# Gated linear attention into a softplus MLP: paired first blocks worked by halves of the heads, and the bias additions moved

## The chip, the cores and the metric

The kernel runs on one core of a Trainium2 chip. The metric is device time in microseconds (us) of one launch; the mean granted clock of TensorE was 0.99 of full or more in every run compared here, unless a run is called slow. Each run was timed beside runs of the kernel before on the same chip.

The engines carry short names in the profile: PE is TensorE (matmul), PEld its weight loads, DVE is VectorE, ACT is ScalarE, POOL is GpSimd, SP is SyncE, which issues the loads and stores. A name such as L474 is line 474 of the kernel that was profiled; the changed kernel has other line numbers for the same work.

## The reference

```python
batch, n_heads, seq, head_dim = (4, 8, 768, 48)      # q, k, v, f_logit: f32
n_tokens, d_model, d_ff = (3072, 384, 2048)          # w_in, w_out: f32

f = 1.0 / (1.0 + np.exp(-f_logit))
for t in range(S):
    state = f[:, :, t, :, None] * state + np.einsum('bhd,bhe->bhde', k[:, :, t], v[:, :, t])
    y[:, :, t] = np.einsum('bhd,bhde->bhe', q[:, :, t], state)
x = y.transpose(0, 2, 1, 3).reshape(B * S, H * D)
h = x @ w_in
g = np.maximum(h, 0.0) + np.log1p(np.exp(-np.abs(h)))
out = (g @ w_out).astype(np.float32)
```

## The kernel before

The 3072 tokens are 24 blocks of 128, six to a batch. Per block the attention is done in chunked form: the cumulative sum of the log gate is a matmul (`cs`), its exponentials scale k and q (`ek`, `eq`, then the products `mk` and `mq`), TensorE transposes the products (`tr`), multiplies them (`p`), VectorE masks the result (`m`, the tile `ptm`), and the output (`o`) is the masked part plus the state's part. The state is carried by `u`, `tt` and `sn`. Then x is transposed (`xt`) and goes through 48 matmuls with w_in (`f1`), exp, ln, and 16 matmuls with w_out (`f2`).

All engines execute their queues in order, and the program decides the order once, when it is built: every piece of work is a task with an engine, a guessed cost, the tasks it needs and a key, and a small list scheduler lays the tasks out. The first four blocks are loaded as two pairs, so that one 384 KB load brings even and odd tokens of two blocks:

```python
def load(n, i):
    b, c = divmod(i, NC)
    if i < PAIRED:
        t = work.tile([128, H, 2, D], FP32, name=n + "2", tag=n + "2", bufs=2)
        nc.sync.dma_start(out=t, in_=SRC[n][b, :, c * T:(c + 2) * T, :].rearrange(
            "h (p e) d -> p h e d", e=2))
        in_t[n, i], in_t[n, i + 1] = t[:, :, 0, :], t[:, :, 1, :]
        return
# ... [cut]
def a_cs2(i, e):                       # one block e of a pair, all heads
    ps = att_bank("cs")
    for k in range(2):
        nc.tensor.matmul(out=ps[:, 0:DM], lhsT=negS if k > e else negB,
                         rhs=z_t[i + k].rearrange("p h d -> p (h d)"), ...)
# ... [cut]
# the tasks of a pair, for each block e of it
task(("mk", i + e), "DVE", MUL, [("ek", i + e), ("k", i)], t + 2, a_mk, (i + e,), "qkp", ...)
task(("mq", i + e), "POOL", MUL, [("eq", i + e), ("q", i), ("mk", i + e)], t + 2.1,
     a_mq, (i + e,))
task(("vb", i + e), "POOL", VB, [("v", i)], t + 3, a_vb, (i + e,), "vb", ...)
# ... [cut]
# weights: each 768 KB quarter is cast in two halves of its columns
task(("cast", n, i, 0), "DVE", COPY, [("at", n, i)], key, cast_w, (n, i, 0))
task(("cast", n, i, 1), "POOL", COPY, [("at", n, i)], key + 0.1, cast_w, (n, i, 1))
# ... [cut]
# a constant from ln 2 times the column sums of w_out is added to every output row
def f_out(i):
    osb = work.tile([128, DM], FP32, name="osb", tag="osb", bufs=16)
    if i < LATE:                       # LATE = 13: copied now, added later on GpSimd
        nc.vector.tensor_copy(out=osb, in_=o_ps.pop(i)[:, 0:DM])
    else:
        nc.vector.tensor_tensor(out=osb, in0=o_ps.pop(i)[:, 0:DM], in1=bias_bc, op=ALU.add)
```

Note the three needs of `mq`: the exponential, the load of q, and `mk` of the same block, which is on another engine and which `mq` does not read.

## Time and profile before

| | before |
|---|---|
| median of the runs beside the changed kernel | 193.49 us (193.43 to 193.71, 4 runs) |
| profiled span | 191.7 us |
| TensorE busy, of it warm-up matmuls | 96%, 135 matmuls |
| first feed-forward matmul starts | 18.94 us |
| share of the chain on TensorE | 86% |

The prediction shows the lines that carry this. Columns: start, time from first start to last end, engine, line, operation, tiles, shapes, count, and in brackets how long the engine stood idle before and what ended that.

```profile
16.17 1.28 POOL L211 CAST vb<-v 128x384 bf16<-128x384 f32 x2 [3.09 <-DMA v<-in_v_dram]
18.14 1.08 POOL L211 CAST w_in_bf<-w 128x768 bf16<-128x768 f32 x1 [0.68 <-DMA w<-in_moe_w_in_dram]
...
20.65 1.84 POOL L282 TENSOR_TENSOR qkp<-q,ee 128x384 bf16<-128x384 f32 x2
```

GpSimd stands idle for 3.09 us at the cast of the second pair's v, which is at the head of its queue and waits for its load. The q products of the same pair stand behind that cast, behind a weight cast and a state update, and run only at 20.65, although the exponentials that they need were done by 15.26.

### The profile page before, as it was taken

The page shows a single profiled execution, that of the slowest core. Times are in us where ns is not written, and L with a number is a line of the kernel's source. Part 1 is how long each engine was busy: PE and PEld are TensorE (multiplying, and loading weights), DVE is VectorE, ACT ScalarE, POOL GpSimd, SP SyncE. Part 2 cuts the span into 40 slices and gives each one's busy share as a digit, 9 for nine tenths or more (in the row PEclk, how much of TensorE's full clock was granted, in tenths as well). Part 3 has the DMA queues.
Part 4 walks back from the last instruction along what each step waited for, and adds up shares of the span by engine and source line. Part 5 has one row for each costly group of instructions (what it writes and reads, how often), then busy time and mean ns, then how long its engine had stood idle before and what let it go on. Part 6 is the DMA issues. An engine that isn't in the chain of part 4 may idle for free.

```text
span 191.7 us, 6346 instructions
## 1 busy us (share of the span) xinstructions
PE 184.8 (96%) x2613; PEld 150.4 (78%) x2613; DVE 126.6 (66%) x274; ACT 149.3 (78%) x249; POOL 108.5 (57%) x154
## 2 busy tenths in 40 slices
PE   6999889999999999999999999999999999999993
PEld 6868678777887887787788788778778778788773
DVE  7847878275979778637777867556866867653011
ACT  3675497898978888899979789779789877766770
POOL 6344967069898699844345444589998533500000
PEclk9999999999999999999999999999999999999999
DMA  6999999999999963854655683687799910110112
GB/s 159 261 270 384 382 374 247 177 190 169 203 168 200 159 119 62 163 119 89 125 112 104 121 160 67 110 159 188 163 299 194 284 50 33 41 46 0 44 41 84
DMA packets 98925, 30.29 MB, mean 158 GB/s; under 512 B 92112, under 2 KB 97360, under 8 KB 98896
## 3 DMA queue, kind: packets, MB, share of 16 engines
q1 hardware_dynamic: 98896, 29.89, 71.5%
q8 instruction: 20, 0.33, 0.8%
q14 instruction: 9, 0.07, 0.1%
HBM read 25.17 MB, written 4.72 MB: 156 GB/s over the span
## 4 chain that ended last, share of the span: by engine, by line
PE 86%; SPq 4%; DMA 4%; POOL 3%; DVE 1%; issue 1%; POOLq 0%
PE hh L474 33%; PE ops L494 32%; PE qkT L296 5%; SPq L141 4%; DMA v<-in_v_dram 4%; PE pp L374 4%; PE oo L446 2%; PE xTp L460 2%; PE cs L257 2%; PE oo L441 2%; PE uu L391 1%; PE ops L501 1%; POOL qkp L282 1%; POOL sst L430 1%; POOL vb L211 1%
## 5 line engine op out<-in xcount | busy, mean ns | idle before, releaser
L474 PE MATMUL hh<-xT,w_in_bf 128*128 128x128 bf16 x1152 | 113.9, 219 | 0.6 <-DVE w_in_bf L211 0.6
L494 PE MATMUL ops<-w_out_bf,gg 128*128 128x384 bf16 x368 | 108.3, 326 | 0.0
L474 PEld LDWEIGHTS <-w_in_bf 128*128 128x128 bf16 x1152 | 87.8, 98 | 21.8 <-DVE w_in_bf L211 0.8
L482 ACT ACTIVATE uexp<-hh 128x512 f32<-128x512 f32 x96 | 56.6, 595 | 22.8 <-PE hh L474 22.0
L488 ACT ACTIVATE gg<-uexp 128x1024 bf16<-128x1024 f32 x48 | 50.7, 1056 | 1.4
L494 PEld LDWEIGHTS <-gg 128*128 128x128 bf16 x368 | 34.9, 98 | 5.2
L383 DVE TENSOR_TENSOR ptm<-pp,mask 128x512 bf16<-128x512 f32 x40 | 25.8, 686 | 7.5 <-PE pp L374 7.4
L278 POOL TENSOR_TENSOR qkp<-kk,ee 128x384 bf16<-128x384 f32 x20 | 18.3, 915 | 20.6 <-ACT ee L270 9.1
L430 POOL TENSOR_TENSOR sst<-tt,ect 48x192 bf16<-48x192 f32 x32 | 16.3, 510 | 19.4 <-DVE tt L421 15.6
L211 DVE COPY qkT<-qkT 128x1024 bf16<-128x1024 bf16 x22 | 15.2, 689 | 17.0 <-PE qkT L296 16.4
L400 DVE STREAM_TRANSPOSE ect<-ee 32x128 bf16<-32x128 bf16 x64 | 19.5, 305 | 2.5 <-ACT ee L274 1.3
L282 POOL TENSOR_TENSOR qkp<-qq,ee 128x384 bf16<-128x384 f32 x20 | 18.4, 918 | 0.0
L211 DVE CAST xx<-oo 128x384 bf16<-128x384 f32 x21 | 11.7, 557 | 6.4 <-PE oo L446 5.6
L233 POOL TENSOR_TENSOR wsum<-wsum,w 128x384 f32<-128x384 f32 x14 | 14.0, 1001 | 0.5
L525 POOL TENSOR_TENSOR osb<-osb,bias_bc 128x384 f32<-128x384 f32 x13 | 12.7, 1005 | 0.9 <-DVE bias_bc L243 0.9
L717 PE MATMUL ops<-negU,ident 128*128 128x128 bf16 x135 | 11.1, 244 | 1.9 <-POOL ident masks.py:199 1.9
L211 POOL CAST vb<-vv 128x384 bf16<-128x384 f32 x20 | 10.1, 507 | 4.5 <-DMA vv<-in_v_dram 4.5
L270 ACT ACTIVATE ee<-cs 128x384 bf16<-128x384 f32 x24 | 11.2, 477 | 1.8 <-PE cs L257 1.0
L521 DVE TENSOR_TENSOR osb<-ops,bias_bc 128x384 f32<-128x384 f32 x10 | 5.6, 558 | 10.5 <-PE ops L494 10.3
L296 PE MATMUL qkT<-ident,qkp 128*128 128x128 bf16 x160 | 12.2, 219 | 0.0
L421 DVE TENSOR_TENSOR tt<-uu,sst 48x192 f32<-48x192 f32 x32 | 11.3, 354 | 0.9
L717 PEld LDWEIGHTS <-ident 128*128 128x128 bf16 x135 | 9.6, 112 | 2.3 <-POOL ident masks.py:199 1.9
(83 smaller groups left out, 211.6 us busy)
## 6 DMA issues: line engine op xcount, KB each, us to landing
ff<-in_f_logit_dram SPq DMA_DIRECT2D x20, 192.0 KB, 4.0
kk<-in_k_dram SPq DMA_DIRECT2D x20, 192.0 KB, 3.8
qq<-in_q_dram SPq DMA_DIRECT2D x20, 192.0 KB, 4.1
vv<-in_v_dram SPq DMA_DIRECT2D x20, 192.0 KB, 4.2
out_dram<-osb SPq DMA_DIRECT2D x19, 192.0 KB, 3.0
w<-in_moe_w_in_dram SPq DMA_DIRECT2D x4, 768.0 KB, 9.2
w<-in_moe_w_out_dram SPq DMA_DIRECT2D x4, 768.0 KB, 8.8
f<-in_f_logit_dram SPq DMA_DIRECT2D x2, 384.0 KB, 5.0
```

The source lines that it names most:

```text
L211: on[eng].tensor_copy(out=out, in_=in_)
L278: on[eng].tensor_tensor(out=qkp_bufs[i % 4][:, H:2 * H, 0:D], in0=in_t.pop(("k", i)), in1=e_bufs[i % 2][:, H:2 * H, 0:D], op=ALU.mult)
L282: on[eng].tensor_tensor(out=qkp_bufs[i % 4][:, 0:H, 0:D], in0=in_t.pop(("q", i)), in1=e_bufs[i % 2][:, 0:H, 0:D], op=ALU.mult)
L296: nc.tensor.transpose(ps[:, a * 128:(a + 1) * 128], qkp[:, a, :], ident)
L383: nc.vector.tensor_tensor(out=ptm_t[i].rearrange("p (a b) t -> p b a t", b=2)[:, half, :, :], in0=p_ps.pop((i, half)).rearrange("p (a t) - ...
L400: nc.vector.transpose(out=t[32 * r:32 * r + 32], in_=e[96:128, 0:NP, 32 * r:32 * r + 32])
L430: on[eng].tensor_tensor(out=sn[lo:hi, :, e0:e0 + D], in0=tt[lo:hi], in1=ec[lo:hi].unsqueeze(2).to_broadcast([48, NP, D]), op=ALU.mult)
L474: nc.tensor.matmul(out=h_ps[i, j // 4][:, j % 4, :], lhsT=w_in_bf[:, r, j * 128:(j + 1) * 128], rhs=xT_t[i][:, r, :], start=(r == 0), stop ...
L482: nc.scalar.activation(out=u_t[i, a // 2][:, 4 * (a % 2):4 * (a % 2) + 4, :], in_=h_ps.pop((i, a)), func=AF.Exp, bias=0.0, scale=1.0)
L488: nc.scalar.activation(out=g_t[i][:, 8 * a:8 * a + 8, :], in_=u_t.pop((i, a)), func=AF.Ln, bias=0.5, scale=0.5)
L494: nc.tensor.matmul(out=o_ps[i][:, 0:DM], lhsT=g_t[i][:, j, :], rhs=w_out_bf[:, j, :], start=(j == 0), stop=(j == NJ - 1), skip_group_check ...
L717: nc.tensor.matmul(out=idle_ps[:, 0:128], lhsT=ident, rhs=negU, start=True, stop=True, skip_group_check=True)
```

## The change

The intent: let the first pairs start on half of f and pass through each step by half of the heads (both blocks of the pair together), so that the chain from load to x is shorter; and take bias work away from GpSimd late in the kernel: 8 outputs instead of 13 get their bias there, one at a time as they come, and the sums of w_out's rows that the bias needs start earlier. Some buffers become fewer. In rewriting the tasks, the change also drops the third need of `mq`. It alters more that the scheduler sees: some guessed costs, a new need among the `exp` tasks, and the engine of some copies and of some set-up work.

```diff
-SUMS = 110
-BIAS = 240
-LATE = 13
+SUMS = 64
+BIAS = 164
+LATE = 8
 ... [cut]
+            if half != 1:
+                in_t[n, i] = work.tile([128, H, 2, D], FP32, name=n + "2", tag=n + "2", bufs=2)
+            hh = slice(0, H) if half is None else slice(4 * half, 4 * half + 4)
+            nc.sync.dma_start(out=in_t[n, i][:, hh], in_=SRC[n][b, hh, c * T:(c + 2) * T, :].rearrange(
                 "h (p e) d -> p h e d", e=2))
-            in_t[n, i], in_t[n, i + 1] = t[:, :, 0, :], t[:, :, 1, :]
 ... [cut]
-    def a_cs2(i, e):
-        ps = att_bank("cs")
-        for k in range(2):
-            nc.tensor.matmul(out=ps[:, 0:DM], lhsT=negS if k > e else negB,
-                             rhs=z_t[i + k].rearrange("p h d -> p (h d)"),
+    def a_cs2(i, a):
+        ps, m = att_bank("cs"), 4 * D
+        for e in range(2):
+            for k in range(2):
+                nc.tensor.matmul(out=ps[:, e * m:e * m + m], lhsT=negS if k > e else negB,
+                                 rhs=z_t[i, a][:, k].rearrange("p h d -> p (h d)"),
 ... [cut: the same for ek, eq, products, transposes, evictions, p, masks, outputs]
-            task(("mq", i + e), "POOL", MUL, [("eq", i + e), ("q", i), ("mk", i + e)], t + 2.1,
-                 a_mq, (i + e,))
+            task(("mq", i, a), "POOL", MUL, [("eq", i, a), ("q", i)], t + 2.1, a_mul2,
+                 (i, a, "q"))
 ... [cut]
-            task(("ev", i, k), "DVE" if k else "ACT", EV, [("tr", i, k, 1)], s + 10.3, a_ev2,
+            task(("ev", i, a), "DVE", EV, [("tr", i, a, 0)], t + 10.3, a_ev2, (i, a), "qkT2",
 ... [cut]
-            task(("add", i), "POOL", 0.95, [("out", i), ("bias out",)], BIAS + 4 * i, add_bias,
+            task(("add", i), "POOL", 0.95, [("out", i), ("bias out",)], BIAS + 4 + 10 * i, add_bias,
 ... [cut]
-        task(("sum", n), "POOL", 1.08, [...], SUMS + 8 * n, add_w, (w, j))
+        task(("sum", n), "POOL", 1.08, [...], SUMS + 6 * n, add_w, (w, j))
-    slots = dict(..., vb=4, qkT=2, qkT2=3, w32=5, ptm=3, xx=2, xT=6, uexp=3, gg=6, osb=16)
+    slots = dict(..., vb=3, qkT=2, qkT2=3, w32=5, ptm=2, xx=2, xT=6, uexp=3, gg=5, osb=12)
```

## The prediction

> **What bounds the kernel now.** I read the page first, then the chain that ended last, then the timelines of the engines up to 33 us, the issue list with the landing of each load, and the start-to-start spacing of the matmuls.
>
> ```profile
> PE 184.8 (96%) x2613; PEld 150.4 (78%) x2613; DVE 126.6 (66%) x274; ACT 149.3 (78%) x249; POOL 108.5 (57%) x154
> PE   6999889999999999999999999999999999999993
> DMA  6999999999999963854655683687799910110112
> PE 86%; SPq 4%; DMA 4%; POOL 3%; DVE 1%; issue 1%; POOLq 0%
> ```
>
> TensorE carries 86% of the chain. The 96% busy flatters it, because early on it runs warm-up matmuls (line 717, 135 of them) that do nothing useful. So I count useful work instead. Back-to-back spacings in the trace are 56 ns for a 128-column matmul, 163 ns for a 384-column one, 43 ns and 25 ns for the 96- and 48-column ones. Counts times spacings give 168.3 us of useful TensorE work in the program. The last matmul ends near 188.6 us, so TensorE falls 20.3 us behind an ideal that starts at zero. Call the clock minus the useful work done by then the lag. It grows in three pieces:
>
> - to 18.94 us, where the first feed-forward matmul starts, only 5.27 us of work is done: lag 13.7;
> - at the tenth transpose of x (32.3 us) 15.24 us is done: lag 17.05, so 3.4 lost in between;
> - from there to the end another 3.3 us over 156 us, some 0.2 us per block, mostly at the p matmuls, which show two gaps of about 0.1 us per block. In 40 to 60 us the excess over nominal spacing is 1.4 us against 0.55 to 0.65 elsewhere.
>
> The chain of waits of 16 to 33 us and the timelines show what the middle piece is:
>
> ```profile
> 8.62 7.43 DMA v<-in_v_dram
> 16.17 1.28 POOL vb L211 x2
> 18.14 1.08 POOL w_in_bf L211
> 19.22 0.78 POOL sst L430
> 20.65 1.85 POOL qkp L282 x2
> 22.55 0.40 PE qkT L305 x4
> ```
> ```profile
> 18.11 0.69 DVE L211 CAST w_in_bf<-w 128x768 bf16<-128x768 f32 x1 [1.02 <-DMA w<-in_moe_w_in_dram]
> 22.47 1.34 DVE L211 CAST w_in_bf<-w 128x768 bf16<-128x768 f32 x1
> 25.50 1.22 DVE L211 CAST w_in_bf<-w 128x768 bf16<-128x768 f32 x1
> 27.40 1.89 DVE L327 TENSOR_TENSOR ptm<-pp,mask 128x512 bf16<-128x512 f32 x3
> ```
> ```profile
> 22.44 1.79 POOL L211 CAST w_in_bf<-w 128x768 bf16<-128x768 f32 x2
> ```
> ```profile
> 18.94 0.68 PE L474 MATMUL hh<-xT,w_in_bf 128*128 128x128 bf16 x9
> ```
>
> The reader should see two things. The first feed-forward matmul follows the cast of the first quarter of w_in, whose load lands at 18.08 us; x of block 0 is transposed and copied by 18.87, at the same moment. And GpSimd does the q products of the second pair only at 20.65, so half of the second weight quarter (landed 20.12) is cast only after 22.44.
>
> **What the Trainium skill says.**
> - "TensorE: Matmul & The Clock Gate", Part 1 (The HAM clock gate): about 107 ns between 128-column matmuls when cold, 56 ns after some 3.4 us of sustained work. The trace agrees: the first 43 warm-up matmuls take 4.34 us (101 ns each), later ones go at 56 ns. The change keeps warm-up matmuls, so I charge nothing for the clock.
> - "SBUF — State Buffer", SBUF: two separate sides: VectorE and GpSimd share a port pair as an exclusive lock. That fits the equal casts of 128x768 on VectorE taking 0.69 to 1.34 us, and a 128x128 copy taking 1.79 us while GpSimd clears buffers. I therefore use 0.7 to 1.2 us for such a cast.
> - "DMA: Bandwidth & Descriptors", Specifications: line rate wants descriptors of 512 B or more. The trace moves about 262 GB/s with the 384 B pieces of the pairs and 370 to 385 GB/s with the weights. The change keeps 384 B pieces, so the weights should land as before.
> - "Perfetto Trace Analysis", Identifying the Most-Contended Engine: matmul busy share is no measure of headroom. This trace agrees, as above.
>
> **The change part by part.**
>
> *Nothing in the total.* Counting matmuls of the changed program at the same spacings gives 168.3 us of useful work again. The cumulative-sum matmuls become twice as many of half the width. Warm-up matmuls fall from 135 to 102. The change can win only lag.
>
> *First pair by halves.* Half of f is 192 KB and should land near 3.7 us instead of 4.43; one half's z steps are two of about 0.5 us instead of four. I step through the new queue orders with the durations of the rows: ek of half 0 near 6.2; k landed 5.93, so mk near 6.8; q landed 7.44, so the q products on GpSimd at 7.5 to 9.3 (0.93 each); copies of qkT to 10.5 (0.69 each); four ptm products (0.69 each) with two small tt steps between, to about 13.9 instead of 16.35; outputs, x and its transposes after that, ready near 16.5 instead of 18.87. But the cast of w_in still cannot start before the landing at 18.08. So the first feed-forward matmul moves from 18.94 to about 18.85, and 2.3 us of the gain dies there.
>
> *What fills the freed time.* In the new order 32 instead of 20 qkp transposes and 48 instead of 32 p matmuls stand before the first feed-forward matmul. That is 12 x 56 ns = 0.67 us plus 16 x 21.5 ns = 0.34 us, together 1.0 us of work done in time that was warm-up. Lag there: 18.85 - 6.28 = 12.6 instead of 13.7.
>
> *From there to the 96th feed-forward matmul* (blocks 0 and 1). GpSimd has only half of vb left, near 19.0, then casts the second quarter on landing, 20.1 to 20.95, instead of 22.4. TensorE: 12 feed-forward matmuls to 19.5, the u products to 20.6, 24 more to 22.0, then quarter 3 (landed 22.11, cast on VectorE by 23.2 and on GpSimd, behind sn, by 23.75), to 24.8. Now VectorE binds: tt to 24.0, cast of quarter 4 (landed 24.18) to 25.4, and only then the last three ptm, to 27.4. The output of the first half of block 2 waits until 26.1 (1.3 us lost), that of the second half until 27.4 (0.4 lost). The rest runs through, and the 96th feed-forward matmul ends near 30.1. Useful work by the tenth x transpose is then 14.92 us at about 30.25: lag 15.3 instead of 17.05. So the two steps together win 1.75 us, 1.0 of it before the first feed-forward matmul and 0.7 after.
>
> *Blocks 4 on.* Their loads land as before (f of block 4 at 33.39, q at 35.30). In the new order the transposes of block 4 come after 24.0 us of work, at 39.3 with this lag; its q product can end near 38.6. No new wait, but little room.
>
> *Bias and sums.* 8 instead of 13 bias additions on GpSimd remove 5 x 1.005 = 5.0 us there. The evictions of blocks 8 to 12 go from a copy of 0.56 us to an addition of 0.56 us on VectorE. The 15 sums of 1.0 us are the same, only begun elsewhere in its order. GpSimd is 57% busy and off the chain: 0 us on the end. The bias matmul (0.70 us for two passes) moves on TensorE and costs the same.
>
> *Fewer buffers* (gg 6 to 5, osb 16 to 12, ptm and vb 3): 0 if the order holds. *Tail*: same final halves and stores, 0.
>
> Sum: 193.48 - 1.75 = 191.7 us.
>
> **The rivals.**
> 1. *Nothing is gained*: the head is bound by loads, 18 us of 262 to 385 GB/s; what comes early then waits at a cast or a sum. For it: the landing at 18.08 and the loss I find at VectorE. Against: 3.4 us are lost between 19 and 32 although the queue delivers a quarter every 2.05 us, and GpSimd's backlog there is plain. It would give about 193.3.
> 2. *All early gaps close*: from 18.85 on TensorE never waits. Then the lag stays at 12.6 instead of 17.05, a gain of 4.4 and a time of 189.1. Against it: quarters come every 2.05 us, and blocks 0 and 1 hold only 24 x 56 ns = 1.34 us of work for each; other pair-2 work covers only part of the rest.
> 3. *The middle suffers*: bias_bc is now needed by block 8's eviction, right after it is made; with two PSUM banks for the output a late sum would stop TensorE. Also stores wait in the same issue queue as loads. Before, GpSimd in 60 to 80 us was 90% busy (17.98 of 20) with sums and TensorE still did not stop, which speaks against. It would cost 0.5 to 2 us, giving 192 to 194.
>
> **Range and chances.** My walk rests on VectorE casts of 0.7 to 1.3 us, three of them in line, so about 0.7 us either way; the middle adds 0.4. I take 190.4 to 192.8. Faster by over 2% means below 189.6, nearly rival 2 in full: 0.06. Slower by over 2% needs over 197.4: 0.01. Within: 0.93.
>
> **What would show it.** Right: the first feed-forward matmul within 0.3 us of 18.9; 12 more transposes ahead of it; GpSimd's cast of quarter 2 near 20.1; a wait of TensorE for ptm at 25 to 27; lag near 15.3 at the tenth x transpose; the same 0.2 us per block later. Wrong: w_in landing earlier or later by over 0.5 us, TensorE gaps above 0.3 us after 33 us, or an output eviction waiting for bias_bc.

## The result

The changed kernel took 192.02 us (192.00 to 192.51, 4 runs) beside 193.49 us (193.43 to 193.71, 4 runs) of the kernel before. The ratio is 0.9928, with a 95% interval of 0.991 to 0.9946. Ratios in this document are the mean time of one kernel's fast runs over that of the other's of the same rounds, so not quite the ratio of the medians quoted. A gain of 0.7% counts as the same at the threshold of 2%. The predicted 191.7 us was 0.3 us too low, and the time lies within the range.

The page of the changed kernel, the lines that answer to those of before (the first two are its span and busy times by engine, then TensorE's busy tenths in 40 slices, then the shares of the chain that ended last):

```profile
span 190.2 us, 6300 instructions
...
PE 183.8 (97%) x2588; PEld 150.1 (79%) x2588; DVE 125.5 (66%) x272; ACT 148.6 (78%) x247; POOL 106.3 (56%) x150
...
PE   6899899999999999999999999999999999999993
...
PE 85%; SPq 6%; DMA 6%; DVE 1%; issue 0%
```

The span is 1.5 us shorter, and GpSimd, 3% of the chain before, is gone from it. What stands in its place is the load of the weights, shown by the chain of waits between 13 and 50 us:

```profile
13.11 11.60 DMA w<-in_moe_w_in_dram
24.70 0.02 issue
24.72 0.70 DVE w_in_bf L214
25.43 0.05 issue
25.47 0.76 PE hh L518 x9
```

The fourth quarter of w_in lands at 24.70, VectorE casts it in 0.70, and TensorE goes on at once. The timeline of GpSimd shows why it left the chain:

```profile
13.89 1.79 POOL L296 TENSOR_TENSOR qkp<-q,ee 128x384 bf16<-128x384 f32 x2 [0.98 <-ACT ee L291]
15.63 1.61 POOL L474 TENSOR_TENSOR sst<-tt,ec 48x192 bf16<-48x192 f32 x2
17.30 0.51 POOL L214 CAST vb<-v 128x384 bf16<-128x384 f32 x1
18.00 1.08 POOL L214 CAST w_in_bf<-w 128x768 bf16<-128x768 f32 x1 [0.19 <-DMA w<-in_moe_w_in_dram]
19.03 0.50 POOL L214 CAST vb<-v 128x384 bf16<-128x384 f32 x1
20.03 1.08 POOL L214 CAST w_in_bf<-w 128x768 bf16<-128x768 f32 x1 [0.50 <-DMA w<-in_moe_w_in_dram]
```

The q products of the second pair now run at 13.89, nearly 7 us earlier, ahead of the casts of v. From 18 us on, GpSimd waits for the quarters and not they for it (in this profile).

To place the gain I use the prediction's lag: the clock minus the useful TensorE work begun and done by then (counts times spacings; a p matmul of the later blocks counts 42 ns; the bias product, two passes, at its own 0.35 us a pass, which makes the total 168.6 us in both kernels). It is read at four marks: the first feed-forward matmul; the 61st, which is the first that needs the fourth quarter of w_in; the tenth transpose of x; and the start of the last matmul. The lines of TensorE at the first two marks (the first mark of the kernel before is in the prediction, the second of the changed kernel in the chain above):

```profile
26.77 0.34 PE L474 MATMUL hh<-xT,w_in_bf 128*128 128x128 bf16 x3 [0.59 <-DVE w_in_bf L211]
```
```profile
18.88 0.83 PE L518 MATMUL hh<-xT,w_in_bf 128*128 128x128 bf16 x12
```

| lag, us | first f1 | 61st f1 | tenth x transpose | last matmul |
|---|---|---|---|---|
| before | 13.74 | 16.23 | 17.11 | 19.71 |
| changed | 12.65 | 14.75 | 15.76 | 18.36 |
| difference | 1.09 | 1.48 | 1.35 | 1.35 |

Both kernels lose 2.60 us between the third and fourth mark. So the whole gain is made before 31 us, and four fifths of it stand already at the first feed-forward matmul. That share is not fixed: in the profile of the changed kernel's third run, below, where the loads landed later, the difference is only 0.40 us at the first mark and 1.00, 1.05 and 1.05 at the others.

### The profile page after: what moved, and what is told of

Same layout as the page of the kernel before. It is cut to its first block, busy times and chain, and to the rows that moved or that the text cites. A ratio compares the mean times of both kernels' runs of the same rounds, so it can differ in the third digit from the quotient of the medians.

```text
span 190.2 us, 6300 instructions
## 1 busy us (share of the span) xinstructions
PE 183.8 (97%) x2588; PEld 150.1 (79%) x2588; DVE 125.5 (66%) x272; ACT 148.6 (78%) x247; POOL 106.3 (56%) x150
## 4 chain that ended last, share of the span: by engine, by line
PE 85%; SPq 6%; DMA 6%; DVE 1%; issue 0%
PE hh L518 33%; PE ops L538 33%; DMA w<-in_moe_w_in_dram 6%; SPq L143 5%; PE qkT L333 5%; PE pp L418 4%; PE oo L490 2%; PE xTp L504 2%; PE cs L260 2%; PE oo L485 2%; PE uu L435 1%; PE ops L545 1%; SPq L200 1%; PE oo L405 1%; PE biasps L242 0%
## 5 line engine op out<-in xcount | busy, mean ns | idle before, releaser
L538 PE MATMUL ops<-w_out_bf,gg 128*128 128x384 bf16 x368 | 110.3, 326 | 0.0
L214 DVE COPY qkT<-qkT 128x1024 bf16<-128x1024 bf16 x24 | 16.6, 691 | 17.7 <-PE qkT L333 15.5
L565 DVE TENSOR_TENSOR osb<-ops,bias_bc 128x384 f32<-128x384 f32 x15 | 8.4, 558 | 10.6 <-PE ops L538 10.3
L770 PE MATMUL ops<-negU,ident 128*128 128x128 bf16 x102 | 9.6, 249 | 1.9 <-POOL ident masks.py:199 1.9
L333 PEld LDWEIGHTS <-qkp 128*128 128x128 bf16 x160 | 10.4, 98 | 1.2
L214 DVE COPY xT<-xTp 128x384 bf16<-128x384 bf16 x21 | 7.4, 352 | 5.2 <-PE xTp L504 5.2
L252 ACT ACTIVATE ff<-ff 128x384 f32<-128x384 f32 x20 | 10.2, 512 | 0.5 <-DMA ff<-in_f_logit_dram 0.5
```

The costliest lines, as they stand in the source:

```text
L214: on[eng].tensor_copy(out=out, in_=in_)
L333: nc.tensor.transpose(ps[:, a * 128:(a + 1) * 128], qkp[:, a, :], ident)
L538: nc.tensor.matmul(out=o_ps[i][:, 0:DM], lhsT=g_t[i][:, j, :], rhs=w_out_bf[:, j, :], start=(j == 0), stop=(j == NJ - 1), skip_group_check ...
```

## The experiments

Theory H, from the prediction: the work by halves fills time in front of the first feed-forward matmul and moves VectorE's queue; the bias is worth nothing. Rival D: the loads of the weights bound the head, so the time would follow their landing and little else. A third, called Q here, came out of the traces after the first runs: what counts is the place of the second pair's q products in GpSimd's queue. Every kernel gave a correct result. The first four runs below share one chip, the next four a second and the last four a third. The kernel before varied little throughout: 193.36 to 193.74 us in 37 runs.

### The bias part alone

In the kernel before:

```diff
-SUMS = 110; BIAS = 240; LATE = 13
+SUMS = 64;  BIAS = 164; LATE = 8
-    BIAS + 4 * i      (additions)     SUMS + 8 * n      (sums)     osb bufs=16
+    BIAS + 4 + 10 * i (additions)     SUMS + 6 * n      (sums)     osb bufs=12
```

> The kernel before with only the bias part of the change: sums from key 64 every 6, bias at key 164, eight instead of thirteen outputs finished on GpSimd, output buffers 12 instead of 16. My theory (the gain is all in the second pair's work being done earlier around the first weights): 193.4, within 0.2 us of before. Rival B (the gain comes from the bias part, the sums or the buffers): 192.0 to 192.5.

Measured: 193.48 us (193.40 to 193.56), ratio 0.9996 (0.9984 to 1.0008). The lags are 13.93, 16.18, 17.06 and 19.68, those of the kernel before. The bias part is worth nothing on the time.

### The halves alone

In the changed kernel, the bias part put back (`SUMS`, `BIAS`, `LATE`, the two keys and `osb` as before).

> The changed kernel with the old bias part (13 additions on GpSimd, late sums, 16 output buffers). My theory: 192.0, within 0.2 us of the changed kernel. Rival B: 193.0 to 193.5.

Measured: median 192.07 us (191.77 to 193.10, 5 runs), ratio 0.9931 (0.9912 to 0.995). A sixth run, the profiled one, was slow at 197.66 us with a mean clock of 0.974, and is left out; its trace is not used. What is left of the change without its bias part, the halves and the dropped need together, carries the whole gain.

### The second pair's transposes held back

In the changed kernel, the transposes of the second pair are made to stand behind the arrival of the first weight quarter in the order:

```diff
-                     [("mk" if k else "mq", i, a), None if k else ("tr", i, a, 1)],
+                     [("mk" if k else "mq", i, a), None if k else ("tr", i, a, 1),
+                      ("wi", 0) if i else None],
```

> The changed kernel, but in the order the transposes of the second pair stand only after the first quarter of w_in is cast, so the 32 transposes and 16 p matmuls do not run ahead of the first feed-forward matmul; TensorE does 12 more transposes and 16 more p matmuls after it, and VectorE's copies and masks of the second pair come later. My theory: the lag at the tenth x transpose goes from 15.7 back to at least 16.7 and the time is 192.9 to 193.6. Rival C (the gain is the earlier first pair): stays near 192.0, since TensorE idles 1.3 us at the third and fourth quarter anyway and can take the work there.

Measured: 192.88 us (192.12 to 193.41), ratio 0.9963 (0.9946 to 0.9979): about half of the gain is lost. The lags are 14.06, 15.07, 16.86 and 19.04. At the first feed-forward matmul only 4.99 us of useful work is done instead of 6.23, so 1.24 us of work that had lain in front is given up. But by the 61st most of that is made good, 15.07 against 14.75: there the quarters of w_in bound, and the work that was held back fills the waits for them. Then it loses once more: 1.79 us from the second to the third mark instead of 1.01. VectorE's and TensorE's timelines of the held kernel:

```profile
25.21 1.29 DVE L368 TENSOR_TENSOR ptm<-pp,mask 128x512 bf16<-128x512 f32 x2
...
27.18 1.37 DVE L368 TENSOR_TENSOR ptm<-pp,mask 128x512 bf16<-128x512 f32 x2
```
```profile
26.99 0.49 PE L518 MATMUL hh<-xT,w_in_bf 128*128 128x128 bf16 x6 [0.53 <-ACT uexp L526]
```

The masks do come later, the last ends at 28.55 instead of 27.33, but no output of the pair is seen to wait for one. The largest piece of the loss is a wait of TensorE for an `exp` on ScalarE: 0.75 us from one matmul to the next, before 26.99. The forecast held for the lag (16.86, at least 16.7); the time is at the edge of its range. So work ahead of the first quarter is worth something, but not its own length: it is neither "1.24 us lost" nor "0".

### f loaded whole

In the changed kernel, the two loads of half of f become one:

```diff
     def load(n, i, half=None):
+        if half == 1:
+            return
+        half = None
```

> The changed kernel with f of each pair loaded in one piece again instead of two halves: the first exponentials start near 4.5 instead of 3.5 us and x of block 0 is ready some 0.7 to 1.0 us later, still before the first quarter of w_in is cast at 18.7. My theory: the first feed-forward matmul still at 18.9, time 192.0 to 192.4. Rival C (the earlier first pair is what pays): 192.8 to 193.2.

Measured: 192.47 us (191.91 to 193.28, 6 runs), ratio 0.9946 (0.9926 to 0.9967). The profiled run took 191.91 us, with lags of 12.83, 14.72, 15.55 and 18.15, no worse than the changed kernel's. x of block 0 was ready at 17.38 instead of 17.19 us, not 0.7 to 1.0 later: with f in one piece, k landed at 5.84 and q at 7.36, instead of 6.17 and 7.67. The median is 0.45 us higher, but the runs spread by 1.4 us and the intervals overlap. All that follows is that most of the gain stands without the half load.

### The changed kernel again

> The changed kernel once more, for its spread and a second profile. My theory: 192.0 median. The kernels with halves spread over 191.8 to 193.4 in the first call where the kernel before keeps to 193.4 to 193.7. If that is the landing of the third and fourth quarter of w_in reaching TensorE directly (in the kernel before, the fourth quarter lies over 1 us before VectorE gets to it), this run spreads by about 1 us too, and a profile with a later third quarter shows a longer span by up to the same amount.

Measured: 191.81 us (191.77 to 191.84), ratio 0.9911 (0.9898 to 0.9924), on another chip. The forecast spread of about 1 us did not come: the four runs lie within 0.07 us.

### The first weight quarter loaded earlier

In the changed kernel, the load of w_in's first quarter is issued ahead of the second pair's v:

```diff
+    turn.remove(("wi", 0))
+    turn.insert(turn.index(("v", 2)), ("wi", 0))
```

> The changed kernel with the first quarter of w_in loaded ahead of v of the second pair. My theory: the landing is the floor of the first feed-forward matmul, so that starts at 17.3 to 17.9 instead of 18.9; but the third and fourth quarters land as before and TensorE waits there, so the time is 191.6 to 192.4. Rival D (the start of the first feed-forward matmul sets the end): 190.8 to 191.2.

Measured: 191.87 us (191.75 to 192.44), ratio 0.9919 (0.9907 to 0.9931), the same as the changed kernel beside it. The quarter landed at 16.65 instead of 17.95, and its casts were done at 17.56 on VectorE and 17.98 on GpSimd. I had expected the first feed-forward matmul with it, and that was wrong: it started at 18.91. VectorE's and TensorE's timelines say why:

```profile
17.49 0.91 DVE L296 TENSOR_TENSOR qkp<-k,ee 128x384 bf16<-128x384 f32 x1
```
```profile
18.45 0.62 PE L343 MATMUL qkT<-ident,qkp 128*128 128x128 bf16 x8 [0.51 <-DVE qkp L296]
...
18.91 0.83 PE L518 MATMUL hh<-xT,w_in_bf 128*128 128x128 bf16 x12
```

The cast that came early pushed a k product of the second pair back on VectorE, and TensorE's queue has the transposes of that product in front of the first feed-forward matmul. The wait has moved from the load to VectorE. The time is what I had expected, but for another reason, so this run does not decide against rival D.

### One exponential's logarithm moved

TensorE may lose time in the changed kernel because ScalarE frees an output bank late (an `exp` behind a long `ln`). So the first `ln` is moved back in the order:

```diff
-SHIFT = {}
+SHIFT = {("ln", 0, 0): 13}
```

> The changed kernel with one key changed: the first Ln of block 0 queued on ScalarE after the exponentials of blocks 0 and 1 instead of before them, which frees a bank of the first product 1 us earlier; the order then gives TensorE the second quarter of block 1 ahead of the third quarter of block 0. My theory (what is left of the loss is TensorE idle at the third quarter, 0.96 us, while block 1 still has work that is only barred by the full banks): 191.3 to 191.8. If the third and fourth quarters' landing alone sets it: 192.0.

Measured: 192.28 us (191.99 to 192.61), ratio 0.9934 (0.9921 to 0.9946): no gain. The waits in question are gone (the largest spacing left there is 0.24 us): the lag grows by 1.50 us from the first to the second mark, from 13.38 to 14.88, instead of 2.10. From the second to the third, to 15.98, it grows by 1.10, no less than in the changed kernel. This profile started its feed-forward late, at 19.61; against the third run's profile, which started at 19.57, it is 0.08 us ahead at the third mark. Later it loses more: while TensorE goes from 24 to 65 us of useful work (about 40 to 82 us on the clock), the lag grows by 1.94 us, against 1.51 in all three profiles of the changed kernel. What costs that was not looked for.

### The outputs put together again

In the changed kernel, the output of a block of a pair is not split by halves of heads; the state's four matmuls come first, then the sixteen masked ones. The text of `a_o2`, shortened:

```diff
+        if a == 0:            # only takes its bank
+            return
-            for p in range(2):            # state's part, half the heads
+            for p in range(4):            # state's part, all heads
-        for h in range(4 * a, 4 * a + 4):
+        for h in range(H):
```

> The changed kernel with the output of each block of the pairs again made in one go, the four state matmuls and then the sixteen masked ones, instead of by halves. The trace shows 0.11 to 0.14 us at each change between 112-row, 64-row and 128-row matmuls, and halves have six more such changes than whole outputs in the second pair. My theory: the changes cost what the trace shows, but the first half's matmuls fill time before the last mask is done: 191.8 to 192.3. If the halves of the output are worth their early start: 192.4 or more.

Measured: 192.04 us (191.53 to 193.59), ratio 0.9933 (0.9907 to 0.9959): not told apart from the changed kernel. The trace does show the small cost of the split. TensorE in the changed kernel, then in this one (112, 64 and 128 are rows of the matmul):

```profile
26.07 0.25 PE L399 MATMUL oo<-sst,qkT 112*128 112x96 bf16 x2
26.25 0.37 PE L405 MATMUL oo<-vb,ptm 64*128 64x48 bf16 x8
```
```profile
27.11 0.34 PE L400 MATMUL oo<-sst,qkT 112*128 112x96 bf16 x4
27.38 0.57 PE L406 MATMUL oo<-vb,ptm 64*128 64x48 bf16 x16
```

Twice the work of the state's part takes 0.34 instead of 0.25, and of the masked part 0.57 instead of 0.37 us. Not every change of rows costs, as the expectation had it: from 128 to 112 rows and back the spacing stays at 56 and 42 ns, and only changes to or from the 64-row matmuls take 112 to 138 ns. The outputs of the second pair have eight such changes with halves and four when whole. The lag grows by 0.42 us from the second to the third mark, instead of 1.01. In this profile, though, the first quarter of w_in landed at 18.85 instead of 17.95, and the lag began 0.74 us higher; the two nearly cancel.

### The dropped need of the q product, alone

In the kernel before, whole blocks kept:

```diff
-            task(("mq", i + e), "POOL", MUL, [("eq", i + e), ("q", i), ("mk", i + e)], t + 2.1,
+            task(("mq", i + e), "POOL", MUL, [("eq", i + e), ("q", i)], t + 2.1,
```

> The kernel before with one dependency of its order dropped, which the change also dropped: the q product of a paired block no longer stands behind the block's k product. GpSimd then makes the second pair's q products before it casts the first quarter of w_in (at 17 to 19 instead of 20.65 to 22.5) and casts the second quarter on landing. My theory (the second pair's products coming late on GpSimd is what the change removes, halves or not): VectorE casts the fourth quarter near 24.5 instead of 25.5 and the time is 192.3 to 193.0. Rival (it takes the halves): 193.3 to 193.6.

Measured: 194.02 us (193.96 to 194.30), ratio 1.0028 (1.0016 to 1.004): slower, where I had expected it faster. GpSimd's timeline:

```profile
16.47 1.09 POOL L211 CAST vb<-v 128x384 bf16<-128x384 f32 x2 [3.46 <-DMA v<-in_v_dram]
17.52 1.77 POOL L282 TENSOR_TENSOR qkp<-q,ee 128x384 bf16<-128x384 f32 x2
...
20.79 2.74 POOL L211 CAST w_in_bf<-w 128x768 bf16<-128x768 f32 x3
```

The cast of v still stands ahead, GpSimd still idles 3.46 us, and the q products come 3 us earlier than before, but in the place of GpSimd's half of the first weight quarter. That cast goes to 20.79. TensorE's timeline:

```profile
20.41 0.40 PE L305 MATMUL qkT<-ident,qkp 128*128 128x128 bf16 x4 [0.28 <-DVE qkp L278]
...
21.74 1.18 PE L474 MATMUL hh<-xT,w_in_bf 128*128 128x128 bf16 x18 [0.21 <-POOL w_in_bf L211]
```

The pair's transposes, which wait for its products, now stand in front of the first feed-forward matmul; that starts at 21.04, 2.1 us late, and after six TensorE waits for GpSimd's half of the quarter. Dropping the need does not by itself give the order that the changed kernel has.

### The need of the q product put back

In the changed kernel, halves kept:

```diff
-            task(("mq", i, a), "POOL", MUL, [("eq", i, a), ("q", i)], t + 2.1, a_mul2,
+            task(("mq", i, a), "POOL", MUL, [("eq", i, a), ("q", i), ("mk", i, a)], t + 2.1, a_mul2,
```

> The changed kernel with that dependency put back: each half's q product stands behind its k product, which moves the second pair's q products on GpSimd from 13.9 to behind VectorE's k products, the second half behind the cast of the first quarter. My theory: the time goes up by 0.4 to 1.0 us against the changed kernel, to 192.2 to 192.9. Rival (it takes the halves only): within 0.2 us of the changed kernel.

Measured: 193.52 us (192.94 to 193.64), ratio 0.9991 (0.9979 to 1.0003): the whole gain is gone, more than I had expected, with all the work by halves still in place. The changed kernel beside it took 192.29. GpSimd's timeline:

```profile
16.83 0.51 POOL L214 CAST vb<-v 128x384 bf16<-128x384 f32 x1 [3.03 <-DMA v<-in_v_dram]
...
18.46 0.91 POOL L296 TENSOR_TENSOR qkp<-q,ee 128x384 bf16<-128x384 f32 x1
...
20.29 0.91 POOL L296 TENSOR_TENSOR qkp<-q,ee 128x384 bf16<-128x384 f32 x1
```

With the need back, the scheduler puts a cast of v ahead of the q products again, and the idle 3 us of the kernel before return. The q products run at 18.46 and 20.29 instead of 13.89 to 15.67, GpSimd's half of the first weight quarter is cast between them, at 19.31, and the first feed-forward matmul starts at 20.38, behind transposes that waited for the first of these products until 19.42 and behind 13 warm-up matmuls. The lags, 14.72, 16.47, 17.56 and 19.75, are those of the kernel before at the end. Late loads don't explain it: the first quarter landed at 18.84 in this profile, and at 18.85 in that of the whole outputs, which took 192.03 us where this one took 193.35. That also speaks against rival D.

### Both of the order's small losses taken away

In the changed kernel, the outputs whole and the first weight quarter earlier (the two edits above together).

> A try at a better version: the changed kernel with whole outputs of the paired blocks (six changes of row count fewer on TensorE in the second pair, 0.4 us between the 61st feed-forward matmul and the tenth x transpose in the profile of that edit) and with the first quarter of w_in ahead of v of the second pair (no wait for a late first landing). If both hold: 191.3 to 191.6, and a spread below 0.7 us. If they only shift the waits: 191.8 to 192.2.

Measured: 192.36 us (191.75 to 193.07, 5 runs; a sixth, at 195.29 with a mean clock of 0.982, was slow), ratio 0.9934 (0.9915 to 0.9954). Its profile is the shortest of all, 189.9 us, with lags of 13.13, 14.92, 15.50 and 18.10. Two of the runs took 191.75, but the spread is 1.3 us and not below 0.7. No better version is established.

### The changed kernel a third time

> The changed kernel on the same chip as the three beside it: 191.8 to 192.1.

Measured: 192.29 us (191.66 to 193.54), ratio 0.9948 (0.992 to 0.9976). The lags are 13.34, 15.23, 16.06 and 18.66. The kernel is not the steady thing that its first rounds showed: at full clock its runs spread by 1.9 us on this chip, by 0.07 us on another. The chip alone is not the reason, since on that other chip the kernel with whole outputs spread by 2.1 us; nor is the half load, since with f whole the spread was 1.4. The kernel before never did. I have not found the cause. What the traces offer is that landings of the loads move from run to run (the first quarter of w_in between 17.81 and 18.85 us in profiles with the same order of loads), and that the changed kernel waits for them at more places, but no run ties the slow ones to that.

## Why the prediction was right or wrong

**Right, by its steps.**

- *Useful work and warm-up*: unchanged, and 102 warm-up matmuls for 135, as counted.
- *The first pair by halves*: half of f landed at 3.48 (predicted 3.7). x of block 0 was copied by 17.19, later than the predicted 16.5, but still ahead of the cast, so that the miss cost nothing. The first feed-forward matmul started at 18.88 (18.85), with 32 transposes and 48 p matmuls in front as listed. The lag there is 12.65 (12.6).
- *GpSimd's second quarter*: cast at 20.03 to 21.11 (20.1 to 20.95).
- *The middle and the tail*: 2.60 us of lag in both kernels (0 of difference predicted; the size that the prediction gave for this stretch, 3.3 us, is 2.60 by these marks).
- *The bias*: 0 predicted, ratio 0.9996 measured.
- *Its signs of being wrong*: one came up, since the third and fourth quarters landed over 0.5 us later; after 33 us the trace has no gap of TensorE above 0.3 us.

**The size off.** The lag at the tenth x transpose is 15.76 us instead of the predicted 15.3, and the gain 1.35 us instead of 1.75. The step that failed is the walk from the first to the 96th feed-forward matmul. It charged 1.3 and 0.4 us to TensorE waiting for `ptm`, behind VectorE casts of up to 1.2 us and a fourth quarter landed at 24.18. The timelines of VectorE and TensorE of the changed kernel say otherwise:

```profile
22.68 0.69 DVE L214 CAST w_in_bf<-w 128x768 bf16<-128x768 f32 x1 [0.55 <-DMA w<-in_moe_w_in_dram]
...
24.72 0.69 DVE L214 CAST w_in_bf<-w 128x768 bf16<-128x768 f32 x1 [0.71 <-DMA w<-in_moe_w_in_dram]
25.45 1.89 DVE L368 TENSOR_TENSOR ptm<-pp,mask 128x512 bf16<-128x512 f32 x3
```
```profile
23.43 1.60 PE L518 MATMUL hh<-xT,w_in_bf 128*128 128x128 bf16 x24 [0.75 <-DVE w_in_bf L214]
```

The casts took 0.69 us, and VectorE stood idle before each of them, waiting for the load: quarters 3 and 4 landed at 22.66 and 24.70, half a microsecond later than the landings that the prediction took over from the kernel before. TensorE's waits were for the quarters, a spacing of 0.96 us at 22.5 and one of 0.32 us at 25.2; for `ptm` there is one spacing of 0.10 us, at 27.3. The masks did end at 27.3 as predicted, but that is luck, since the later landing and the shorter casts cancel; TensorE reached the outputs late enough hardly to wait. What else the walk left out is the change to and from matmuls of 48 and 64 rows; between the first and third mark these changes add some 1.4 of the 3.1 us of lag, and the split doubles those of the outputs; with the outputs whole the growth from the second to the third mark fell from 1.01 to 0.42 us.

**What the prediction did not name.** It split the gain into 1.0 us before the first feed-forward matmul and 0.7 after, as if each could be had alone. Measured were 1.09 and 0.26 in the first profile, and 0.40 and 0.65 in that of the third run. The held-back kernel shows that they are not additive: it gave up 1.24 us of work in front and was only 0.3 us behind at the 61st matmul, and 0.7 at the end by its trace. And it credited the early work to the halves. It saw that GpSimd did the q products late in the kernel before, but took the new order as given, without asking what made it. The run with the need of `mq` put back answers: in the kernel by halves one dropped need in the order, nothing in the data, decides whether a cast that waits for its load stands at the head of GpSimd's queue. The Trainium skill, "TensorE: Matmul & The Clock Gate", Part 1 (Architectural detail), says of the queues that "ACT/DVE are strict FIFO; GPSIMD is per-Q7 strict FIFO". The traces agree: GpSimd idled 3.09, 3.46 and 3.03 us in three kernels in front of that cast, with other work queued behind it.

**The rivals.** Rival 1 (nothing gained, the loads bound the head) fell as a total, since 1.35 us were gained with the first quarter landing 0.13 us earlier than before; but it was right that loads bind the stretch from 19 to 25 us. Rival 2 (all gaps close, 4.4 us) fell for the reason given against it: TensorE runs out of work between the quarters. Rival 3 (the middle suffers) fell with the bias run.

**What stays open.** Whether the halves are needed at all: the kernel before with its q products placed ahead of the casts of v, whole blocks kept, was not run; dropping the need alone did not bring about that order. The scheduler's changed guesses and the copies moved to other engines were not tried apart from the halves either. And what makes the kernels by halves spread.

## What to carry to other kernels

When engines work through fixed queues, look for an instruction that waits for a load at the head of a queue with ready work behind it: here the splitting of every step gained nothing while such a cast stood in front. When a scheduler decides the order, a dependency that no data requires is a decision about the order, so list such dependencies among the parts of a change, and test each alone and put back; here neither the dropped need nor the halves gained anything alone, so that either test by itself would have misled. Work moved ahead of a bound is worth only what does not fit into the waits behind it, so do not add the gains of two stages that share the same filler.

## What the Trainium skill lacked or had wrong

- "TensorE: Matmul & The Clock Gate", Part 2 (Back-to-back issue gap), gives about 81 ns per matmul for a sustained stream of weight loads and matmuls of 128 columns. Here the 1152 such pairs of the feed-forward run at 56 ns from start to start at full clock, each with its own weight load; the measurement decides.
- "TensorEngine Tiling (Array Packing)", Key Properties, says that changing the tiling mode drains TensorE, but gives no figure. Here a change to or from matmuls of 48 or 64 rows took 95 to 152 ns from start to start (259 ns after a 384-column matmul, where 162 ns is usual), and 25 to 56 ns is the spacing within the groups of 48 to 128 columns; between 112 and 128 rows a change cost nothing (56 and 42 ns). That this is the drain is not shown. Splitting the outputs of two blocks in halves cost part of 0.6 us by that.
- No page that I read gives how far landings of the same loads scatter from run to run. In the seven fast profiles of kernels with the same order of loads, the k of the first pair landed between 6.17 and 7.06 us and the first quarter of w_in between 17.81 and 18.85 us, on a kernel whose whole gain is 1.4 us.
